# A first batch whose fills are ordered behind its chain: two turned copies, one Square and the routing of three query units

## The chip, the cores and the metric

The kernel runs on one core of a Trainium2 chip. A core has five engines that run their own queues of instructions side by side: TensorE (PE, matmuls; its weight loads are listed apart as PEld), VectorE (DVE), ScalarE (ACT), GpSimd (POOL) and SyncE (SP, which here issues the loads). In the traces of this kernel each queue is worked off in the order in which it was written at build time; an instruction whose inputs are not there yet holds up all that stands behind it on its engine. The metric is the device time of one execution in microseconds, median of the runs.

## The reference, cut to what matters

The shapes are B = 4 batches, N = 11456 tokens of C = 128 numbers, 49 agents, and 8 experts of 128 x 1024 and 1024 x 128 weights.

```python
def sm(a, b):
    s = scale * (a @ b.transpose(0, 2, 1))
    e = np.exp(s - s.max(-1, keepdims=True))
    return e / (e.sum(-1, keepdims=True) + 1e-09)
agent_v = sm(agents, k) @ v                 # 49 rows per batch
x = (sm(q, agents) @ agent_v).reshape(B * N, C)
...
xn, en = x / |x|, expert_emb / |expert_emb|
logits = xn @ en.T / tau
expert_idx, gate_w = argmax(logits), softmax(logits) at it
out = gate_w * (relu(x @ w1[expert_idx]) @ w2[expert_idx])
```

Every x of a batch is a mix of the same 49 rows of agent_v, so nearly all tokens of a batch go to one expert, and the kernel works with `w1.T @ agent_v` (1024 x 49) in place of `w1`. Tokens for which that does not hold are done again at the end.

## The kernel before, in words

Work on keys and queries goes by units of 1024 tokens (8 columns of 128; `NU` = 12 per batch, the last one short). The feed-forward layers go by tiles of 512 tokens (`ffn_mm1`, `ffn_mm2`, `ffn_out`), two to a unit.

`first()` runs the first batch up to the point where its tokens can flow: all key units (`k1_f32`: transposes into PSUM `fTp`, copies to `fT`, scores `sp`, running maximum `m_run`), all value units, the agents' values (`av_chain`), then the **chain** of `pick_expert(0)`. Around the chain stand **fills**, which it does not need: four query units of the first batch (`q_unit(0, 0..3)`, `LEAD` = 4) and six key units of the second batch (`k1_f32(1, 0..5)`).

The chain, with the names that the rows carry: `gp` = w1 times the agents' values on PE; the Square of `w1s` on ACT with its sum (`sel,wsq`), summed over partitions by PE (`total`) and made into a scale on DVE (`hsc`, `sgw`); `gts` = the scaled `gp`, on ACT; from it a key for each of the 1024 hidden columns (`mean`, `pw` over ACT's squares `sel<-gts`, several small steps on `key`, `uid`); `sel<-ident,key` spreads the keys on a diagonal (L729, "the diagonal" below); `row` is PE's product that puts all keys in each partition, copied by ACT; four comparisons on DVE (L747) and four Signs on ACT (L749) count each column's `rank`; eight `sel<-iotaf,rank` (L755) make a selection; `placed` (L763, two times eight matmuls) takes the 256 columns that matter in order, giving `gh` and `gl`. Then `second()` (Square of `w2s` with its sum, a scale, a scaled copy), `linp` and `w2pp`, which give `lin` and `w2p`. With `gh`, `gl` the first layer (`hp`) can start, with `lin`, `w2p` the second (`yp`).

A query unit: transposes and scores as for keys, `qe` (exp), halves in `e_0`/`e_1`, a transpose of them by PE (`tp`, f32 units only, that is the four of `LEAD`), ACT's **turned copy** `tt<-tp`, then **routing**: PE's `rtp` (16 pairs of matmuls), `rtg`, products and sums (`rt`, `qq`) on DVE and POOL, and per group of units (unit 0, units 1 and 2, ...) a row of small steps (`route_group`: `nrm` with a power on POOL, `cc`, `lga`, `ex`, `esa`, `el`, `gs`).

The order of each engine's queue is made at build time by a scheduler that goes by its own timeline and by priorities; `tc.high_priority()` puts a stretch of code ahead, and

```python
    def in_place(last):

        return tc.issue_after(last[-1].ins) if last else nullcontext()
```

keeps what is written inside it behind a given instruction. SP's queue alone is written by hand. Tiles are reused: four PSUM buffers `h` (`fTp`, `tp`, `rtp`, `hp`), two `s` (`sp`), one `rt` buffer for all units.

Of the kernel before, what the change touches and what calls it, by code (L numbers as in the profile page):

```python
# [13 lines left out]
AF = mybir.ActivationFunctionType  # L14
# [4 lines left out]
P = 128  # L19
# [10 lines left out]
def kernel(ctx: ExitStack, tc: tile.TileContext, q, k, v, agents, emb, tau, w1, w2, out):  # L30
    nc = tc.nc
    pe, dve, act, pool, sp = nc.tensor, nc.vector, nc.scalar, nc.gpsimd, nc.sync

    B, N, C = q.shape
    A = agents.shape[1]
    E, D, F = w1.shape
    NF = F // P
# [52 lines left out]
    def psh(name):  # L90
        return ps_h.tile([P, 512], F32, name=name, tag="h")
# [103 lines left out]
    for b in range(B):  # L195
        t_ = pss("aT")
# [91 lines left out]
    gts = cst.tile([P, NF, 2, LO], F32, name="gts")  # L288
    gt16 = cst.tile([P, 2, NF, 2, LO], F16, name="gt16")
    sel = cst.tile([P, NF, FW], F16, name="sel")  # L290
# [79 lines left out]

    DMA_STEPS = 10
    y_log = []
    y_last, h_last, p_last, q_last = [], [], [], []
    h_slots = slots(XS)
    x_slots, s_slots, d_slots, e_slots, t_slots, qe_slots = slots(XB), slots(NU), slots(len(kds)), slots(len(e16)), slots(TB), slots(LEAD)

    def in_place(last):

        return tc.issue_after(last[-1].ins) if last else nullcontext()
# [248 lines left out]
    def pick_expert(b, g):  # L628

        bt = batches[b]  # L630
# [19 lines left out]
        w1s, w2s = load_expert(e0i)  # L650
# [41 lines left out]
        if b > 0:  # L692
            yield 1
            gp = first_layer()
        act.activation(gts[:, :, :, :A], gp[:, : NF * A].rearrange("p (c a) -> p c a", a=A).unsqueeze(2).broadcast_to([P, NF, 2, A]), AF.Copy, scale=sgw)
        yield g

        def second():

            act.activation(w2x[:, :, 0], w2s, AF.Square, accum_out=sq[1])  # L700
            s3, i3 = yield from half_scale(total(sq[1], psx), 6, "w2")
            yield g
            act.activation(w2x[:, :, 0], w2s, AF.Copy, scale=s3)
            if b > 0:
                pool.tensor_tensor(out=w2s, in0=w2s, in1=s3.unsqueeze(2).broadcast_to([P, NF, D]), op=ALU.mult)
                pool.tensor_tensor(out=w2x[:, :, 1], in0=w2s, in1=w2x[:, :, 0], op=ALU.subtract)
            return s3, i3
# [51 lines left out]
        def placed(h, w):  # L759
            t_ = psx("placed")[:, :w]  # L760
            with in_place(y_last):
                for c in range(NF):
                    pe.matmul(out=t_, lhsT=gt16[:, h, c].rearrange("p h a -> p (h a)"), rhs=sel[:, c, :w],  # L763
                              start=(c == 0), stop=(c == NF - 1))
            return t_

        gmx = sm.tile([P, 2], F32, name="gmx", tag="gmx")
# [24 lines left out]
        t_ = psx("linp")  # L792
# [62 lines left out]
    def q_unit(b, u, g):  # L855
        bt = batches[b]
        p, n = ushape(u)
        yield from here(("q", b, u))
        tt_of[b, u] = yield from take(t_slots, len(checks(b, u)) + sum(unit_of(t)[0] == u for t in range(NT)))
        f32 = b == 0 and u < LEAD  # L860
        i = yield from take(x_slots)
        with in_place(p_last) if p_last else behind(asked["q", b, u]):
            xT = pe_T(units["q", b, u], p, n)
        used("q", b, u)
        yield g[0]
        s = pss("sp")
        scores(s, xT, b, p, n)
        give(x_slots, i)
        spv = s[:p, : n * A].rearrange("p (c a) -> p c a", a=A)
        mx = sm.tile([P, UJ], F32, name="qmx", tag="qmx")[:p, :n]  # L870
        dve.tensor_reduce(out=mx, in_=spv, axis=AX.X, op=ALU.max)
        ie = yield from take(qe_slots)
        e = wk.tile([P, UJ, A], F32, name="qe", tag="qe", bufs=LEAD)[:p, :n]
        dve.tensor_tensor(out=e, in0=spv, in1=mx.unsqueeze(2).broadcast_to([p, n, A]), op=ALU.subtract)  # L874
        yield g[1]
        act.activation(e, e, AF.Exp, scale=SCALE)
        yield g[2]
        i = yield from take(e_slots)
        e2 = e16[i % len(e16)]
        hi = e2[:p, :n, :A]  # L880
        i_ = act.copy(hi, e)  # L881
        if not ffn_at[0]:
            q_last[:] = [i_]
        (dve if f32 else pool).tensor_tensor(out=e2[:p, :n, LO : LO + A], in0=e, in1=hi, op=ALU.subtract)  # L884
        tt = wk.tile([P, UJ * P], F16, name="tt", tag="tt", bufs=TB)
        if f32:
            tp = psh("tp").bitcast(F16)
            for c in range(n):
                pe.transpose(out=tp[:, c * p : (c + 1) * p], in_=e2[:p, c, :], identity=ident16[:p, :p])
            act.copy(tt[:, : n * p], tp[:, : n * p])  # L890
        else:
            if ffn_at[0]:
                yield 4
            sp.dma_start_transpose(out=tt[:, : n * p].rearrange("k (c p) -> k c p", p=p),
                                   in_=e2[:p, :n, :].rearrange("p c k -> p (c k)"))
        give(e_slots, i)
        yield g[3]
        tts[b, u] = tt
        while not hasattr(bt, "r_hi"):
            yield 1  # L900
        s = (pss if ffn_at[0] else psh)("rtp")
        with in_place(y_last):
            for c in range(n):
                o = s[:p, c * RW : (c + 1) * RW]
                pe.matmul(out=o, lhsT=tt[:, c * p : (c + 1) * p], rhs=bt.r_hi, start=True, stop=False)
                pe.matmul(out=o, lhsT=tt[:, c * p : (c + 1) * p], rhs=bt.r_lo, start=False, stop=True)
        gi = group_of[u]
        us = groups[gi]
        if (b, gi) not in rtgs:
            rtgs[b, gi] = wk.tile([P, GC, E + 1], F32, name="rtg", tag="rtg", bufs=4)  # L910
        if not hasattr(bt, "qq"):
            bt.qq = sm.tile([P, 2, NCOL], F32, name="qq", tag="qq")
        rtg, qq = rtgs[b, gi], bt.qq
        c0 = ucol(u) - ucol(us[0])
        cs = slice(c0, c0 + n)
        if p < P:
            pmem(rtg[p:, cs], 1.0)
            pmem(qq[p:, :, ucol(u) : ucol(u) + n], 1.0)
        sv = s[:p, : n * RW].rearrange("p (c w) -> p c w", w=RW)
        rt = wk.tile([P, 2, UJ, A], F32, name="rt", tag="rt", bufs=1)[:p, :, :n]  # L920
        act.copy(rtg[:p, cs], sv[:, :, : E + 1])
        pool.tensor_tensor(out=rt[:, 1], in0=e, in1=e, op=ALU.mult)
        dve.tensor_tensor(out=rt[:, 0], in0=sv[:, :, E + 1 :], in1=e, op=ALU.mult)  # L923
        give(qe_slots, ie)
        yield 1
        pool.tensor_tensor(out=rt[:, :, :, : A // 2], in0=rt[:, :, :, : A // 2], in1=rt[:, :, :, A // 2 + 1 :], op=ALU.add)  # L926
        yield g[4]
        dve.tensor_reduce(out=qq[:p, :, ucol(u) : ucol(u) + n], in_=rt[:, :, :, : A // 2 + 1], axis=AX.X, op=ALU.add)
        routed[b, gi] = routed.get((b, gi), 0) + 1
        if routed[b, gi] == len(us):  # L930
            spawn(route_group(b, gi, sum(ushape(x)[1] for x in us)), 1, half=True)
# [520 lines left out]
    def first():  # L1452
# [38 lines left out]
        yield from fetch(two)  # L1491
        for u in range(2):
            spawn(q_unit(0, u, (1, 0, 0, 1, 0)))
        while len(tts) < 2:
            yield 1
        p_last.clear()
        with tc.high_priority():
# [179 lines left out]
```

## Time and profile before

| | us |
|---|---|
| median of 3 runs (lowest, highest) | 740.89 (738.49, 745.61) |
| profiled execution, its own time | 741.78 |
| its span from first to last instruction | 740.0 |
| outside the span | 1.78 |
| PE busy in the span | 688.6 |
| mean granted clock of TensorE, share of full | 0.972 |

The page gives busy times of the engines and the chain that ended last. A view by stretches of time (windows) gives busy time of each engine and the granted clock in each; the timeline lists the instructions of one engine in order, with the idle time ahead of each and what ended it. A matmul in f32 stands as two rows in the trace where the program has one, so 16 `sp` of one unit are x32. Starts are what queues are read by: ends of matmuls are modelled.

### The profile page before, as it was taken

To read this page: it belongs to the slowest core of one execution; us is meant where nothing else is said; L and a number is where in the kernel's file an instruction comes from. 1 tells how busy PE (TensorE), PEld (TensorE's weight loads), DVE (VectorE), ACT (ScalarE), POOL (GpSimd) and SP (SyncE) were. 2 spreads that over 40 slices of the span, in tenths; PEclk is the share of its full clock that TensorE was granted. 3 is DMA by queue.
4 is the path that set the end of the run, shared out by engine and by line. 5 is a ranking of instruction groups with operands and counts; after the bars stand their busy time and mean duration, and the time that the engine had idled before them with its cause. 6 is when DMAs were issued, how large, how long until landed. Compare 5 with 4: busy or idle time off the path is not lost.

```text
span 740.0 us, 23507 instructions
## 1 busy us (share of the span) xinstructions
PE 688.6 (93%) x9416; PEld 574.9 (78%) x9416; DVE 568.1 (77%) x1499; ACT 475.6 (64%) x1161; POOL 338.8 (46%) x576
## 2 busy tenths in 40 slices
PE   8997889989978899999999889989999999999996
PEld 6886678867867788788888778878897776787675
DVE  4676887864457999988558998965658899789886
ACT  3436858667457757877758837865669447766772
POOL 5003401572245557655615836565638356255410
PEclk9998999999969999999999999999999999999998
DMA  8986239846389786598659439945452247223211
GB/s 329 278 306 215 94 73 249 187 137 197 95 205 342 154 199 166 148 279 214 160 158 268 112 67 253 287 124 159 135 172 94 81 87 194 62 60 115 61 45 64
DMA packets 157817, 122.59 MB, mean 166 GB/s; under 512 B 78727, under 2 KB 134105, under 8 KB 157707
## 3 DMA queue, kind: packets, MB, share of 16 engines
q1 hardware_dynamic: 144331, 97.44, 51.1%
q10 hardware_dynamic: 13120, 23.47, 9.1%
q8 instruction: 74, 1.21, 0.7%
q14 instruction: 36, 0.29, 0.1%
q0 software_dynamic: 256, 0.17, 0.1%
HBM read 79.14 MB, written 23.72 MB: 139 GB/s over the span
## 4 chain that ended last, share of the span: by engine, by line
PE 56%; DVE 23%; DMA 6%; ACT 5%; issue 4%; POOL 4%; SPq 0%; ACTq 0%; POOLq 0%; DVEq 0%
PE sp L430 8%; PE fTp L417 6%; PE avp L521 6%; PE hp L1168 4%; PE hp L1169 4%; PE yp L1192 3%; PE yp L1201 3%; DVE hh L1178 3%; PE yp L1204 3%; PE yp L1206 3%; PE yp L1205 3%; PE vp L1017 3%; DMA kt<-in_k_dram 2%; DVE ot L1220 2%; DMA xq<-in_q_dram,ix 1%
## 5 line engine op out<-in xcount | busy, mean ns | idle before, releaser
L1026 ACT ACTIVATE vp<-vp 128x512 f32<-128x512 f32 x191 | 112.3, 588 | 31.7 <-PE vp L1014 16.3
L1178 DVE SCALAR_TENSOR_TENSOR hh<-hp,hh 128x512 f16<-128x512 f32 (+1 forms) x147 | 98.4, 675 | 24.5 <-ACT hh L1177 23.9
L1204 PE MATMUL yp<-w2p,hh 128*128 128x128 f16 (+1 forms) x582 | 109.9, 220 | 0.0
L1205 PE MATMUL yp<-w2p,hh 128*128 128x128 f16 (+1 forms) x582 | 109.8, 220 | 0.0
L1206 PE MATMUL yp<-w2p,hh 128*128 128x128 f16 (+1 forms) x582 | 108.5, 220 | 0.0
L1177 ACT ACTIVATE hh<-hp 128x512 f16<-128x512 f32 (+1 forms) x147 | 85.1, 587 | 34.9 <-PE hp L1169 28.7
L430 PEld LDWEIGHTS sp<-aT_all,fT 128*64 128x64 f32 (+1 forms) x2400 | 83.7, 140 | 23.2 <-issue 11.5
L430 PE MATMUL sp<-aT_all,fT 128*64 128x49 f32 (+1 forms) x2400 | 97.6, 228 | 3.8 <-DVE qe L874 1.4
L1168 PE MATMUL hp<-tt,gh 128*128 128x512 f16 (+1 forms) x207 | 77.5, 377 | 4.3 <-DVE fT L420 2.4
L1169 PE MATMUL hp<-tt,gl 128*128 128x512 f16 (+1 forms) x207 | 77.8, 378 | 0.0
L965 POOL TENSOR_TENSOR nrm<-qq,half 128x16 f32<-128x16 f32 (+2 forms) x28 | 70.4, 2515 | 0.3
L884 POOL TENSOR_TENSOR e<-qe,e 128x392 f16<-128x392 f32 (+1 forms) x44 | 38.1, 866 | 68.0 <-ACT e L881 67.8
L1220 DVE TENSOR_TENSOR ot<-yp,gs 128x512 f32<-128x512 f32 (+1 forms) x92 | 61.1, 670 | 9.3 <-PE yp L1206 3.7
L1201 PE MATMUL yp<-w2f,hh 128*128 128x128 f32 (+1 forms) x456 | 66.7, 284 | 0.0
L1192 PE MATMUL yp<-lin,tt 128*128 128x128 f16 x720 | 63.3, 221 | 2.9 <-DVE w2p L810 1.4
L1204 PEld LDWEIGHTS <-hh 128*128 128x128 f16 (+1 forms) x582 | 57.6, 99 | 10.3 <-issue 0.5
L422 ACT COPY fT<-fTp 128x512 f32<-128x512 f32 (+1 forms) x87 | 48.6, 563 | 24.7 <-PE fTp L417 17.9
L1206 PEld LDWEIGHTS <-hh 128*128 128x128 f16 (+1 forms) x582 | 57.5, 99 | 8.1 <-issue 1.5
L1205 PEld LDWEIGHTS <-hh 128*128 128x128 f16 (+1 forms) x582 | 57.4, 99 | 5.8 <-issue 0.3
L1201 PEld LDWEIGHTS yp<-w2f,hh 128*128 128x128 f32 (+1 forms) x456 | 58.9, 194 | 2.9 <-issue 1.1
L926 POOL TENSOR_TENSOR rt<-rt 128x384 f32<-128x384 f32 (+1 forms) x48 | 40.5, 843 | 45.1 <-DVE rt L923 42.0
L417 PE MATMUL fTp<-ident,qt 128*128 128x128 f32 x360 | 57.0, 288 | 3.3 <-ACT fT L422 1.1
(373 smaller groups left out, 1786.3 us busy)
## 6 DMA issues: line engine op xcount, KB each, us to landing
kt<-in_k_dram SPq DMA_DIRECT2D x44, 512.0 KB, 6.6
vt<-in_v_dram SPq DMA_DIRECT2D x44, 512.0 KB, 6.2
qt<-in_q_dram SPq DMA_DIRECT2D x44, 512.0 KB, 5.5
out_dram<-ot ACTq DMA_DIRECT2D x88, 256.0 KB, 3.4
w1s<-in_moe_w_dram SPq DMA_DIRECT2D x8, 512.0 KB, 4.6
w2s<-in_moe_w_dram SPq DMA_DIRECT2D x8, 512.0 KB, 5.6
tt<-e SPq DMA_TRANSPOSE x44, 4.1
kt<-in_k_dram SPq DMA_DIRECT2D x4, 96.0 KB, 5.8
```

What stands on the lines that cost most here:

```text
L417: pe.transpose(out=tp[:, c * p : (c + 1) * p], in_=src[:p, c0 + c, :], identity=ident[:p, :p])
L430: pe.matmul(out=s[h : h + w, c * A : (c + 1) * A], lhsT=xT[:, c * p + h : c * p + h + w], rhs=aT_all[:, b, :], start=True, stop=True, skip ...
L1026: act.activation(z[:p], z[:p], AF.Relu, scale=-1.0, accum_out=bt.vsum[:p, at : at + 1])
L1168: pe.matmul(out=hp[:, :m], lhsT=bt.gh[:, fs], rhs=tt, start=True, stop=False)
L1169: pe.matmul(out=hp[:, :m], lhsT=bt.gl[:, fs], rhs=tt, start=False, stop=True)
L1177: h_last[:] = [act.activation(hh[:, :m], hp[:, :m], AF.Relu)]
L1178: dve.scalar_tensor_tensor(out=hl[:, :m], in0=hp[:, :m], scalar=0.0, in1=hh[:, :m], op0=ALU.max, op1=ALU.subtract)
L1192: pe.matmul(out=yp[:p, c, :], lhsT=tc_, rhs=bt.lin[:, h], start=(c == 0 and h == 0), stop=False, skip_group_check=True)
L1201: y_last[:] = [pe.matmul(out=y, lhsT=hh[:, cs], rhs=bt.w2f[:, f], start=False, stop=last, skip_group_check=True)]
L1204: pe.matmul(out=y, lhsT=hh[:, cs], rhs=wh, start=False, stop=False, skip_group_check=True)
L1205: pe.matmul(out=y, lhsT=hh[:, cs], rhs=wl, start=False, stop=False, skip_group_check=True)
L1206: y_last[:] = [pe.matmul(out=y, lhsT=hl[:, cs], rhs=wh, start=False, stop=last, skip_group_check=True)]
```

## The change

It makes three edits, all of which concern the first batch alone.

1. The instruction that makes `gts` is kept in `bt.marks`. The turned copies of the four f32 query units, and in batch 0 the Square of `w2s`, are written behind it on ACT.
2. The last `placed` matmul is kept in `bt.placed`. The `rtp` matmuls of query units 1 to 3 are written behind it on PE (unit 0 stays free).
3. Since the turned copies now wait for the chain, `first()` goes on to the chain when the first two units have their casts (`cast`), no longer when they have their turned copies (`tts`).

```diff
-        act.activation(gts[:, :, :, :A], gp[:, : NF * A].rearrange("p (c a) -> p c a", a=A).unsqueeze(2).broadcast_to([P, NF, 2, A]), AF.Copy, scale=sgw)
+        i_ = act.activation(gts[:, :, :, :A], gp[:, : NF * A].rearrange("p (c a) -> p c a", a=A).unsqueeze(2).broadcast_to([P, NF, 2, A]), AF.Copy, scale=sgw)
+        bt.marks = [i_]
...
-            act.activation(w2x[:, :, 0], w2s, AF.Square, accum_out=sq[1])
+            with in_place(bt.marks if b == 0 else []):
+                act.activation(w2x[:, :, 0], w2s, AF.Square, accum_out=sq[1])
...
-                    pe.matmul(out=t_, lhsT=gt16[:, h, c].rearrange("p h a -> p (h a)"), rhs=sel[:, c, :w],
-                              start=(c == 0), stop=(c == NF - 1))
+                    i_ = pe.matmul(out=t_, lhsT=gt16[:, h, c].rearrange("p h a -> p (h a)"), rhs=sel[:, c, :w],
+                                   start=(c == 0), stop=(c == NF - 1))
+            bt.placed = [i_]
...
+            cast.append(u)
...
         if f32:
+            while not hasattr(bt, "marks"):
+                yield 1
...
-            act.copy(tt[:, : n * p], tp[:, : n * p])
+            with in_place(bt.marks):
+                act.copy(tt[:, : n * p], tp[:, : n * p])
...
+        while f32 and u > 0 and not hasattr(bt, "placed"):
+            yield 1
         s = (pss if ffn_at[0] else psh)("rtp")
-        with in_place(y_last):
+        with in_place(bt.placed if f32 and u > 0 else y_last):
...
-        while len(tts) < 2:
+        while len(cast) < 2:
             yield 1
```

What stands in the queues changes only in the first third of the program: SP's queue is the same row for row, and PE, DVE, ACT and POOL come back to the order of before after 23 to 30 in 100 of their rows; from the product `placed` for the matrix `vm` on the differences are shifts by a few rows.

ACT around `gts` before, from the cast of the second query unit on (`sel,wsq<-w1s` is the Square of w1, `w1s,wsq<-w2s` that of w2, `tt<-tp` a turned copy):

```order
L881 CAST e_1_150<-qe 128x8x49
L688 ACTIVATE sel,wsq_1030<-w1s 128x1024
L700 ACTIVATE w1s,wsq_1031<-w2s 128x8x128
L890 COPY tt<-tp 128x1024
L921 COPY rtg<-rtp 128x72
L695 ACTIVATE gts<-gp,sgw 128x16x49
L921 COPY rtg<-rtp 128x72
L711 ACTIVATE sel<-gts 128x392
L733 CAST gt_152<-gts 128x16x49
```

and now, in the same place (the first turned copy stood two rows further up before):

```order
L884 CAST e_1_150<-qe 128x8x49
L688 ACTIVATE sel,wsq_965<-w1s 128x1024
L422 COPY fT<-fTp 128x512 x2
L695 ACTIVATE gts<-gp,sgw 128x16x49
L897 COPY tt<-tp 128x1024 x2
L702 ACTIVATE w1s,wsq_966<-w2s 128x8x128
L713 ACTIVATE sel<-gts 128x392
L735 CAST gt_152<-gts 128x16x49
```

Two turned copies and the Square of w2 moved from ahead of `gts` to the place between `gts` and its squares, and two copies of query transposes moved ahead of it.

PE before, ahead of and between the first `placed` matmuls (`kt` are keys of the second batch):

```order
L417 MATMUL fTp<-ident,kt 128x128 x4
L430 MATMUL sp<-aT_all,fT 64x49 x8
L417 MATMUL fTp<-ident,kt 128x128 x4
L430 MATMUL sp<-aT_all,fT 64x49 x8
L417 MATMUL fTp<-ident,kt 128x128 x4
L763 LDWEIGHTS gt_152
L763 MATMUL placed<-sel,gt_152 128x256
```

and now, from the last fill ahead of `row` to the first of the sixteen `placed`, which follow each other:

```order
L915 LDWEIGHTS tt
L915 MATMUL rtp<-r_lo,tt 128x58
L430 MATMUL sp<-aT_all,fT 64x49 x25
L742 MATMUL row<-sel,ones 128x512 x2
L765 LDWEIGHTS gt_152
L765 MATMUL placed<-sel,gt_152 128x256
```

Between `row` and the first `placed` stood before eight `tp`, 32 `rtp` matmuls, the transposes of three key units and the scores of one and a half, and between the sixteen `placed` further ones. Now nothing stands there, and all of it comes behind the sixteenth `placed`, ahead of the first `yp`. From the second `tp` group of the stretch to the first `yp` PE has the same set of matmuls in both orders, but for one small `mT`.

DVE now, from the diagonal to the rank (`cc` takes POOL's `nrm`, `esa` ACT's `ex`, `gs` POOL's `el`):

```order
L731 TENSOR_TENSOR sel<-ident,key 128x1024
L733 TENSOR_SCALAR nkey<-key 128x8
L877 TENSOR_TENSOR qe<-sp,qmx 128x392
L937 TENSOR_REDUCE qq<-rt 128x2x8
L406 COPY m_run<-sp 128x392
L888 TENSOR_TENSOR e_1_150<-qe,e_1_150 128x8x49
L983 RECIPROCAL cc<-nrm 128x8
L749 TENSOR_SCALAR sel,rank<-sel,key 128x1024 x2
L991 TENSOR_REDUCE esa<-ex 128x8
L749 TENSOR_SCALAR sel,rank<-sel,key 128x1024
L998 RECIPROCAL gs<-el 128x8
L749 TENSOR_SCALAR sel,rank<-sel,key 128x1024
```

The sum `qq` of unit 0 and the steps `cc`, `esa`, `gs` of group 0 stood ahead of the comparisons before, `qq` and `cc` even ahead of the diagonal; now `cc` stands right ahead of the four comparisons and `esa` and `gs` between them.


## Rows read from the trace of the kernel before

**Rows 1.** The chain that ended last, two pieces: start us, us, what

```profile
64.70 0.94 ACT gts L695
...
90.52 0.98 PE placed L763 x8
```

**Rows 2.** Windows: stretch, length, busy us (instructions) of PE, PEld, DVE, ACT, POOL; clock, DMA

```profile
61.90:102.30 40.40, 34.45 (x472) 27.60 (x472) 34.49 (x95) 31.45 (x63) 15.78 (x27) 0.94 0.25 84
109.00:300.00 191.00, 178.17 (x2528) 150.31 (x2528) 139.73 (x321) 127.61 (x307) 89.67 (x150) 0.96 0.75 195
300.00:740.00 440.00, 416.96 (x5577) 346.63 (x5574) 350.87 (x948) 290.47 (x739) 220.44 (x347) 0.99 0.54 141
```

**Rows 3.** Windows again, short ones, for the granted clock (third figure from the end)

```profile
50.00:53.00 3.00, 3.00 (x16) 3.00 (x17) 1.28 (x6) 0.58 (x1) 0.00 (x0) 0.50 0.52 209
53.00:54.00 1.00, 1.00 (x10) 0.98 (x10) 0.38 (x2) 0.56 (x1) 0.00 (x0) 0.84 0.85 180
60.00:61.00 1.00, 0.00 (x0) 0.00 (x0) 0.00 (x0) 0.91 (x3) 0.00 (x0) 0.57 0.99 401
62.00:67.00 5.00, 4.70 (x51) 4.55 (x50) 2.64 (x10) 4.71 (x11) 1.69 (x5) 0.50 0.02 9
67.00:68.00 1.00, 1.00 (x9) 0.71 (x7) 1.00 (x3) 0.85 (x2) 0.69 (x1) 1.00 0.00 0
```

**Rows 4.** Timeline of PE: start us, us, line, out<-in, count, idle before it and releaser

```profile
61.87 1.03 PE L889 MATMUL tp<-ident,e 128*128 128x128 f16 x8 [2.76 <-DVE e L884]
...
63.35 0.56 PE L252 MATMUL total<-wsq,ones 128*128 128x1 f32 x2
...
65.15 2.98 PE L417 MATMUL fTp<-ident,qt 128*128 128x128 f32 x16
...
72.96 1.14 PE L430 MATMUL sp<-aT_all,fT 128*64 128x49 f32 x32 [1.35 <-DVE qe L874]
...
76.14 1.98 PE L740 MATMUL row<-sel,ones 128*128 128x512 f32 x4 [0.51 <-DVE sel L729]
...
90.45 1.05 PE L763 MATMUL placed<-sel,gt 128*128 128x256 f16 x8
...
102.29 0.23 PE L1192 MATMUL yp<-lin,tt 128*128 128x128 f16 x1 [1.43 <-DVE w2p L810]
```

**Rows 5.** Timeline of ACT, the same columns

```profile
62.28 1.06 ACT L700 ACTIVATE w1s<-w2s 128x1024 f16<-128x1024 f32 x1
...
63.33 0.99 ACT L890 COPY tt<-tp 128x1024 f16<-128x1024 f16 x1
...
64.70 0.93 ACT L695 ACTIVATE gts<-gp,sgw 128x784 f32<-128x784 f32 x1 [0.25 <-DVE sgw L691]
```

**Rows 6.** Timeline of DVE, the same columns

```profile
65.66 0.56 DVE L712 TENSOR_REDUCE mean<-gts 128x8 f32<-128x392 f32 x1 [0.34 <-ACT gts L695]
...
74.87 1.21 DVE L729 TENSOR_TENSOR sel<-ident,key 128x1024 f32<-128x1024 f32 x1
...
78.78 1.28 DVE L747 TENSOR_SCALAR_CACHE_REDUCE sel<-sel,key 128x1024 f16<-128x1024 f32 x1 [1.60 <-ACT sel L741]
...
87.48 1.94 DVE L755 TENSOR_SCALAR sel<-iotaf,rank 128x256 f16<-128x256 f16 x6
...
91.70 0.42 DVE L771 CAST gl<-placed 128x256 f16<-128x256 f32 x1
```

**Rows 7.** Source line L755 within 80:95: duration ns min/median/max, first and last start

```profile
L755 DVE TENSOR_SCALAR sel<-iotaf,rank x8: 273/274/958, 84.6 to 89.1; 128x256 f16<-128x256 f16 x8
```

**Rows 8.** Timeline of POOL, the same columns

```profile
67.31 0.84 POOL L922 TENSOR_TENSOR rt<-qe 128x392 f32<-128x392 f32 x1 [0.87 <-DVE qq L928]
...
71.12 0.20 POOL L969 TENSOR_TENSOR nrm<-ls,nrm 128x8 f32<-128x8 f32 x1
...
84.59 0.87 POOL L926 TENSOR_TENSOR rt<-rt 128x384 f32<-128x384 f32 x1 [0.80 <-DVE rt L923]
...
88.31 2.94 POOL L965 TENSOR_TENSOR nrm<-qq,half 128x16 f32<-128x16 f32 x1
```

More of the change, by code (lines that the diff above doesn't have):

```diff
@@ L372 @@
     y_log = []
-    y_last, h_last, p_last, q_last = [], [], [], []
+    y_last, h_last, p_last, q_last, cast = [], [], [], [], []
     h_slots = slots(XS)
```

## The prediction, made before the result was known

> **What bounds the kernel now.** I read the stretches first, then the chain, then the four timelines of the first batch. PE is busy 688.6 of 740 us, so the question is where it stands still. Behind 109 us it idles 12.8 us of 191 and 23.0 of 440 [rows 2]. In the stretch that the change reorders, from PE's second group of turned transposes (61.87) to its first `yp` (102.29) [rows 4], it is busy 34.45 of 40.40 us [rows 2]: 5.95 us idle. The chain that ended last runs through this stretch by way of `gts` and `placed` [rows 1]. Two readings are possible. The chain of the first batch sets when tokens flow; and the fills put around it keep PE at work while DVE and ACT do the chain. The change shortens the first and moves the second, so the sum has to count both. I take as measure the start of the first `yp`, since the set of matmuls ahead of it is the same in both orders.
>
> **Up to `gts`: about 1.0 us later.** ACT loses a turned copy between the two casts, so the second cast, the half that waits for it and the second `tp` group come about 0.45 earlier: 61.4. But PE now puts eight query transposes where seven routing columns stood, ahead of `total`. Sixteen take 2.98 us [rows 4] over a rise of the clock; at the lower level, with the three key and query halves of 50 to 53 us [rows 3] as a check, eight are 1.6 us. `total` starts near 63.9 (63.35 before [rows 4]), and the second query copy, which ACT has ahead of `gts`, waits for four more transposes, to 65.25, and takes 0.6. `gts` starts near 65.75, against 64.70 [rows 5].
>
> **From `gts` to the diagonal: 9.2 us against 10.2.** DVE is full from `mean` to the diagonal, 65.66 to 74.87 [rows 6]. Seven pieces of routing and copying leave this run (two `qq`, one `rt`, one query copy, one `qe`, `cc`, `esa`) and `rmx` joins: five of them are of the size of `mean` (0.56 us [rows 6]), two are small; some 2.6 us less. ACT takes part of that back: two turned copies (0.99 each) and the Square of w2 (62.28 to 63.33, 1.05) [rows 5] now stand between `gts` and its squares, some 2.9 us, and `pw` waits 0.6 us for them; the half of unit 2, which DVE has ahead of the last key step, waits 1 us for a cast that is as late. So the diagonal starts near 74.9, as before (74.87). Bounds: 74.2, if `gts` loses only 0.3; 75.6.
>
> **From the diagonal to `placed`: little gained, and PE stands still.** `row` follows the diagonal by 1.27 us (76.14 to 74.87) [rows 4, 6]: 76.2. Ahead of it PE has 24 transposes, `tp`, `total`, the scores of three units and one unit's routing. With 3 us for 16, 1.14 for one unit's scores [rows 4] and 2 for the rest that is 9.9 us from 61.4, so of 14.8 us it idles **4.9** (0.5 and 1.35 of such waits stood there before). Then nothing stands between `row` and `placed`, and `placed` needs the selection, the selection the rank, the rank four comparisons and four Signs.
>
> The comparisons started at 78.78 [rows 6]. Now `cc` stands ahead of them on DVE and wants POOL's power of unit 0's sum. Before, POOL's first step after that sum started at 67.31 and the last step ahead of `cc` at 71.12 with one foreign 0.9 us piece between [rows 8]; so `cc` comes some 3.3 us after the sum, which ends near 77.2: 80.5. Four comparisons of 1.28 us [rows 6] follow, each with a short read of its sum, with `esa` and `gs` between: the rank is ready near 86.3, the eight selections (1.94 us for six [rows 6]) take until 88.9, and `placed` ends near 90.3, where the last group started at 90.45 and its copy `gl` at 91.70 [rows 4, 6]. The chain gains about 1 us there, at best 3.5 (no wait for `cc`, PE at full clock).
>
> One selection took 958 ns, the others 274 [rows 7]; it started with a POOL addition that ran from 84.59 for 0.87 us [rows 8]. I take 8 x 0.32 = 2.6 us, since POOL has nothing to do there now. The Trainium skill ("SBUF — State Buffer", section "SBUF: two separate sides") says that VectorE in some modes and GpSimd lock one port pair in turn and that the loser "fully blocks". The first selection agrees with that; by that rule alone the later six, beside a POOL instruction of 2.94 us [rows 8], would have stood still too, and with one more such block the rank's end would come 0.7 later.
>
> PE meanwhile idles from the end of `row` (78.0) to the first selection (86.8): **8.8 us**, where fills stood before. If the clock falls in the idle time ahead of `row`, `row` itself takes up to twice its 1.98 us [rows 4], the comparisons start near 81.1, and the idle time is 6.9 of work at the lower level and waiting alike; the end is the same within 0.5. The level fell to 0.50 about a microsecond into the 2.76 us wait of 59 to 61.9 and was back at 67 [rows 3, 4]: after the new wait I count 1.2 us for the second spell, bounds 0 and 2.5.
>
> The Trainium skill ("TensorE: Matmul & The Clock Gate", section "Part 4: PE-mode transpose") says that PE transposes do not bring the full clock. Here the level rose between 53 and 54 us when PE had done sixteen transposes in a row and one small product since 50.6 [rows 3], so the trace speaks against it. By the rule `gts` would come 0.4 us later still, and the first `yp` as much.
>
> **The first `yp`.** 61.4 (start) + 34.45 (the same work) + 4.9 + 8.8 (idle) + 1.2 (second spell of low clock) + 1.4 (the wait for `w2p`, 1.43 before [rows 4]: DVE still has seven selections for `vm` ahead of it) − 0.3 (`mT`, now later) − 0.5 (the spell of low clock and the waits of `placed` for its selections overlap) = 111.4. I take **111.2, 8.9 us later than 102.29** [rows 4]. Everything that was taken out from between `row` and `placed` (routing, transposes and scores of five units) now stands ahead of the first layers, so a `placed` that is 1 us earlier buys nothing. Bounds: +4.4 (`placed` at 88.0 and no low clock) and +11.5.
>
> **Behind it.** From the product for `vm` on the queues are as before, so the delay is carried on; loads move with it (SP's order is unchanged, and the DMA engines have room: busy for 0.25 of their time in the stretch [rows 2]). PE's 35.9 us of idle time behind 109 [rows 2] can swallow some where the wait is for a transfer or for POOL work that was not pushed back; the waits that I can name hang on queues that are pushed back as a whole. I take a tenth off: **+8.0**, bounds of the share half and none. The profiled execution took 741.78, 0.9 over the median 740.89 of the runs; the sum is a difference, and set on the median it gives **749.0**.
>
> **Rivals.**
> (a) *The debt is swallowed in part.* PE's idle time of 109 to 300 us, 12.8 us [rows 2], belongs for the most part to the second batch's chain on DVE, ACT and POOL; if that chain is not pushed back with PE, half of the delay is lost there: +2.5 to +6, about 745. For it: the second batch's chain, like the first's, is a row of small steps on DVE and ACT. Against: the chain begins with a product of all value units, which PE does in order.
> (b) *The chain wins* (the other side). If what decides is when `gh`, `gl` are there, the seven pieces less on DVE bring `placed` from 91.5 to 88.0, and key fills behind it find room later: −3.5, about 737.4. It needs `cc` to be ready when the row copies are (79 us) and over 8 us of debt to be swallowed; the order shows the fills ahead of the first layers, which speaks against it.
> (c) *Worse still:* `cc`, `gs` and the second group's power (2.94 us [rows 8]) hold DVE again between `placed` and `w2p`, the first `yp` comes at 114 or later: +12, 753.
>
> **How the numbers follow.** A measurement of this kernel can tell about 1 per cent, 7.4 us, from no change: the three runs lie within 7.1 us. My forecast (+6 to +11.5, 747 to 752.4) gets 0.62, (a) 0.24, (b) 0.06, (c) 0.08. The forecast lies on both sides of 748.3; some two thirds of it and (c) are slower by over 1 per cent, 0.52; faster by over 1 per cent would need over twice what (b) gives, 0.03; the rest is 0.45. The range leaves out (b) and the top of (c): 743.5 to 752.8.
>
> **What would show it.** Right: `gts` later than 64.7; PE idle for 7 us or more between `row` and `placed`, with the granted clock at 0.50 in 82 to 87; `cc` on DVE waiting for POOL ahead of the first comparison; `gl` between 88.5 and 92; the first `yp` near 111, and the same distance between the two traces at 200, 300 and 700 us. Wrong: a first `yp` before 106, or a distance that shrinks by more than 3 us between 110 and 300.

## The result, and the profile after

| | before | with the change |
|---|---|---|
| median of 20 runs (lowest, highest), us | 741.43 (737.73, 745.61) | 745.53 (742.61, 749.34) |
| ratio, 95% interval | | 1.006 (1.0042 to 1.0079) |
| profiled execution, its span | 741.78, 740.0 | 745.83, 744.1 |
| mean granted clock | 0.972 | 0.965 |

Slower by 4.1 us, between 3.1 and 5.9. One run of e3, 752.79 us, over 1.5 per cent above the fastest of its kernel, counts as slow and is left out of its numbers. The kernel before was timed again beside each group of runs (medians 740.53 to 741.63), and a ratio is to the runs beside it. The page of the changed kernel: busy time by engine, and the granted clock in 40 slices.

```profile
PE 689.4 (93%) x9416; PEld 574.6 (77%) x9416; DVE 567.7 (76%) x1499; ACT 475.6 (64%) x1161; POOL 340.2 (46%) x576
...
PEclk9996799999978999999999999999999999999999
```

PE has the same work. The fourth and fifth slices (56 to 93 us) hold two spells of low clock, about 58 to 71 and 78 to 88 us; the kernel before has one there, 60 to 67 [rows 3]. Windows of the changed kernel between the second `tp` group, `row`, the end of `placed` and the first `yp`:

```profile
58.64:73.33 14.69, 13.67 (x146) 11.78 (x146) 9.21 (x27) 8.55 (x16) 2.72 (x4) 0.57 0.36 119
73.33:87.27 13.94, 5.58 (x24) 3.29 (x25) 11.06 (x34) 7.59 (x15) 4.02 (x9) 0.68 0.00 1
87.27:105.90 18.63, 18.63 (x304) 16.14 (x302) 11.35 (x29) 15.29 (x30) 9.51 (x15) 0.97 0.29 92
```

The same three stretches of the kernel before, which together are the stretch of [rows 2]:

```profile
61.87:76.14 14.27, 11.20 (x170) 9.86 (x171) 11.75 (x34) 10.00 (x21) 8.09 (x14) 0.82 0.34 116
76.14:91.50 15.36, 13.91 (x188) 10.66 (x190) 13.48 (x36) 12.80 (x26) 6.51 (x9) 1.00 0.35 111
91.50:102.29 10.79, 9.37 (x115) 7.10 (x116) 9.25 (x28) 8.68 (x18) 1.17 (x5) 1.00 0.01 2
```

The case is in these rows. From `row` to the end of `placed` PE's instructions fell from 188 to 24, and the stretch became only 1.4 us shorter (15.36 to 13.94). Behind `placed` they rose from 115 to 304, and that stretch became 7.8 us longer, with PE busy in all of it. PE's timeline of the changed kernel has the idle time (rows that answer to [rows 4]):

```profile
55.67 0.62 PE L895 MATMUL tp<-ident,e 128*128 128x128 f16 x8
58.64 1.03 PE L895 MATMUL tp<-ident,e 128*128 128x128 f16 x8 [2.35 <-DVE e L888]
...
61.17 0.42 PE L252 MATMUL total<-wsq,ones 128*128 128x1 f32 x2
...
73.33 1.98 PE L742 MATMUL row<-sel,ones 128*128 128x512 f32 x4 [1.02 <-DVE sel L731]
83.67 3.60 PE L765 MATMUL placed<-sel,gt 128*128 128x256 f16 x16 [8.35 <-DVE sel L757]
...
105.90 0.62 PE L1201 MATMUL yp<-lin,tt 128*128 128x128 f16 x8
...
107.00 0.22 PE L1213 MATMUL yp<-w2p,hh 128*128 128x128 f16 x1 [0.48 <-DVE w2p L813]
...
114.02 0.39 PE L1029 MATMUL vp<-vm,tt 128*128 128x64 f16 x8 [0.64 <-DVE vm L835]
```

DVE and ACT of the changed kernel (answering to [rows 5, 6]):

```profile
71.83 1.44 DVE L731 TENSOR_TENSOR sel<-ident,key 128x1024 f32<-128x1024 f32 x1
...
77.81 0.20 DVE L983 RECIPROCAL cc<-nrm 128x8 f32<-128x8 f32 x1 [1.84 <-POOL nrm L978]
77.93 1.23 DVE L749 TENSOR_SCALAR_CACHE_REDUCE sel<-sel,key 128x1024 f16<-128x1024 f32 x1
...
83.14 1.65 DVE L757 TENSOR_SCALAR sel<-iotaf,rank 128x256 f16<-128x256 f16 x8
...
87.30 0.42 DVE L774 CAST gl<-placed 128x256 f16<-128x256 f32 x1 [0.37 <-PE placed L765]
```

```profile
63.07 0.94 ACT L695 ACTIVATE gts<-gp,sgw 128x784 f32<-128x784 f32 x1
```

PE's queue is the same in both programs up to the first `tp`, and yet that starts 2.8 us earlier with the change. So all distances are taken from it. In the trace of before it stands at 58.49, and a wait for a load, with slower products behind it, says why:

```profile
8.45 1.54 PE L417 MATMUL fTp<-ident,kt 128*128 128x128 f32 x8 [1.75 <-DMA kt<-in_k_dram]
...
58.49 0.62 PE L889 MATMUL tp<-ident,e 128*128 128x128 f16 x8 [0.28 <-DVE e L884]
```

Starts minus the start of the first `tp`, us, with a second trace of each kernel (e7 and e8, below); `foldp` is the first product of the agents' values of batches 2 to 4, "last" the last row of PE's timeline:

| | gts | row | placed | first yp | first vp | foldp 2 | foldp 3 | foldp 4 | last |
|---|---|---|---|---|---|---|---|---|---|
| before | 6.2 | 17.7 | 27.5 | 43.8 | 50.5 | 143.9 | 319.4 | 474.7 | 673.9 |
| before, e7 | 6.2 | 18.3 | 29.1 | 45.4 | 52.1 | 145.5 | 321.0 | 474.5 | 675.9 |
| change | 7.4 | 17.7 | 28.0 | 50.2 | 58.4 | 150.2 | 327.9 | 481.3 | 680.3 |
| change, e8 | 7.3 | 17.4 | 27.7 | 49.9 | 58.0 | 149.8 | 326.1 | 481.7 | 680.7 |

The first pair of traces is 6.4 us apart at the first `yp` and at the end, the second 4.4 and 4.8. The delay is made between `row` and the first `yp` and is carried through the whole program, though it swings by up to 3 us from mark to mark (7.9 and 5.9 at the first `vp`).

### The profile page after: what moved, and what is told of

It is laid out like the page before. It is cut to its first block, busy times and chain, and to the rows that moved or that the text cites. A ratio compares the mean times of both kernels' runs of the same rounds, so it can differ in the third digit from the quotient of the medians.

```text
span 744.1 us, 23511 instructions
## 1 busy us (share of the span) xinstructions
PE 689.4 (93%) x9416; PEld 574.6 (77%) x9416; DVE 567.7 (76%) x1499; ACT 475.6 (64%) x1161; POOL 340.2 (46%) x576
## 4 chain that ended last, share of the span: by engine, by line
PE 52%; DVE 27%; DMA 6%; issue 5%; POOL 5%; ACT 4%; SPq 0%; ACTq 0%; POOLq 0%; DVEq 0%
PE sp L430 7%; PE fTp L417 7%; PE avp L521 6%; DVE hh L1187 3%; PE hp L1177 3%; PE hp L1178 3%; PE yp L1201 3%; DVE sel L749 3%; PE yp L1215 2%; PE yp L1213 2%; PE yp L1214 2%; DVE ot L1229 2%; PE yp L1210 2%; PE vp L1026 2%; PE placed L765 2%
## 5 line engine op out<-in xcount | busy, mean ns | idle before, releaser
L1213 PE MATMUL yp<-w2p,hh 128*128 128x128 f16 (+1 forms) x582 | 108.9, 219 | 0.5 <-DVE w2p L813 0.5
L1214 PE MATMUL yp<-w2p,hh 128*128 128x128 f16 (+1 forms) x582 | 108.8, 219 | 0.0
L1215 PE MATMUL yp<-w2p,hh 128*128 128x128 f16 (+1 forms) x582 | 107.2, 219 | 0.1
L1229 DVE TENSOR_TENSOR ot<-yp,gs 128x512 f32<-128x512 f32 (+1 forms) x92 | 61.1, 669 | 10.3 <-PE yp L1210 3.6
L888 POOL TENSOR_TENSOR e<-qe,e 128x392 f16<-128x392 f32 (+1 forms) x44 | 38.1, 866 | 67.4 <-ACT e L884 67.2
L935 POOL TENSOR_TENSOR rt<-rt 128x384 f32<-128x384 f32 (+1 forms) x48 | 40.5, 844 | 50.5 <-DVE rt L932 47.7
```

The source lines that it names most:

```text
L1213: pe.matmul(out=y, lhsT=hh[:, cs], rhs=wh, start=False, stop=False, skip_group_check=True)
L1214: pe.matmul(out=y, lhsT=hh[:, cs], rhs=wl, start=False, stop=False, skip_group_check=True)
L1215: y_last[:] = [pe.matmul(out=y, lhsT=hl[:, cs], rhs=wh, start=False, stop=last, skip_group_check=True)]
```

## The experiments

The theory (A): edit 2 takes PE's fills out of the time that DVE and ACT need between `row` and `placed`; PE stands still there and does them later. The main rival (B): the turned copies and the Square of w2, which now stand between `gts` and its squares on ACT, are the price. A third (C): the low clock that follows the idle time.

**e1: edit 2 undone.**

```diff
-        while f32 and u > 0 and not hasattr(bt, "placed"):
-            yield 1
         s = (pss if ffn_at[0] else psh)("rtp")
-        with in_place(bt.placed if f32 and u > 0 else y_last):
+        with in_place(y_last):
```

> The change without its second edit: turned copies and the Square of w2 stay behind gts, but the routing of units 1 to 3 is free again, and the queue has 16 rtp, 16 tp, 12 groups of key transposes and most of their scores between row and placed. Theory A (the price is PE standing still between row and placed, because edit 2 took the fills out): idle time of PE between row and the first placed under 2 us in place of 8.35, first yp 44 to 46 us behind the first tp (43.8 before, 50.2 with the change), time 739 to 743 us. Theory B (the price is the two turned copies and the Square on ACT between gts and its squares, or a gts that comes later): nothing is won back, 744 to 747 us, diagonal and row as late as with the change.

Measured 739.15 us, ratio to before 0.9978 (0.9957 to 1.0000). Its window from `row` to the end of `placed`, and its first `yp`:

```profile
73.18:88.55 15.37, 12.58 (x168) 10.06 (x164) 14.78 (x37) 13.94 (x30) 11.87 (x19) 1.00 0.31 86
```

```profile
98.89 0.61 PE L1198 MATMUL yp<-lin,tt 128*128 128x128 f16 x8 [0.87 <-DVE lin L800]
```

168 instructions stand in the gap again, the clock is full, and the first `yp` comes 43.3 behind the first `tp` (55.58). PE's idle time there is 2.8 us, not under 2 as expected, and the first `yp` a little earlier than the 44 to 46 expected. B is out: ACT has the turned copies and the Square where the change has them, `gts` starts at 7.3 as with the change, and the loss is gone. Edit 2 costs 745.53 − 739.15 = 6.4 us (4.9 by e12); by the ratios, which take each kernel against its own neighbours, 6.1 and 5.2.

**e2: edit 2 alone** (the lines of e1 the other way, on the kernel before).

> Edit 2 alone: turned copies and the Square as before, the routing of units 1 to 3 behind the last placed. The queue then has nothing between unit 0's routing and row, and nothing between row and placed: the transposes of two query units, key work and scores of three units all stand behind. Theory A: PE idles some 8 us ahead of row and some 8 us ahead of placed, the first yp comes 54 to 60 us behind the first tp, time 748 to 756 us. Theory B: gts and diagonal come as before or earlier, placed 2 to 4 us earlier, and the time is 738 to 742 us. A third possibility, the delay being swallowed behind the first yp: idle times as in A and a time of 743 to 747.

Measured 751.53 us, 1.0144 (1.0103 to 1.0185). Its PE:

```profile
68.87 3.67 PE L740 MATMUL row<-sel,ones 128*128 128x512 f32 x4 [7.60 <-DVE nkey L731]
79.06 3.57 PE L763 MATMUL placed<-sel,gt 128*128 128x256 f16 x16 [6.52 <-DVE sel L755]
...
116.62 0.58 PE L1023 MATMUL vp<-vm,tt 128*128 128x64 f16 x8 [0.64 <-DVE vm L833]
```

The chain is much shorter: `row` 13.2 behind the first `tp` (55.67) and `placed` 23.4, 4.1 earlier than before. The first `vp` is at 61.0, 10.5 later, and the kernel 11 us slower (751.53 − 740.53, the median of before beside it). (Its first `yp` came at 38.1, not at the 54 to 60 expected: it is one early group, and most of the work that stood ahead of it before comes behind it, so `vp` is the mark here.)

**e3: the turned copies alone** (edits 1 and 3 without the Square and without edit 2).

> Edit 1 for the turned copies with edit 3, without the Square and without the routing; the Square of w2 stands ahead of the query copies again. Theory A: fills stand between row and placed as before; time 739 to 743 us, and the same as the change without edit 2 within 1.5. Theory B: two thirds of the price of ACT's three instructions is left, 743 to 746 us.

Measured 744.61 us (median of eleven runs), 1.0051 (1.0024 to 1.0078): a miss for A, and by its number B's. But its first `vp` comes at 105.84, 50.0 behind the first `tp`, as in e1 (50.3), and `foldp` 2 at 143.6 in both. The loss comes later: 1.7 us over e1 at `foldp` 3, 3.4 at `foldp` 4, 3.6 at the end. Unlike e1, whose PE queue is that of before again after 16 in 100 of its rows, this one differs up to half of the program, and there PE has a wait that the other traces lack:

```profile
333.94 0.59 PE L1173 MATMUL hp<-tt,gh 128*128 128x512 f16 x1 [2.69 <-DVE hh L1183]
```

Between 240 and 340 us behind the first `tp` PE idles 4.5 us in all, in e1 1.45. So this run says little about ACT in the first batch; what it shows is a small edit there that goes with another order up to half of the program, and with a loss of some 3 us over 200 us further on. That the order makes the loss is a reading of these waits; no run tests it.

**e4: the clock held up.** On the changed kernel, behind the second `row` product:

```diff
+            if b == 0 and h == 1:
+                t_ = psx("warm")
+                with in_place([i_]):
+                    for _ in range(26):
+                        pe.matmul(out=t_, lhsT=ident16, rhs=ident16.unsqueeze(1).broadcast_to([P, 4, P]), start=True, stop=True)
```

> The change, with 26 matmuls of 512 f16 columns on a constant between row and the first placed on PE, whose result nobody reads. They take 5.5 us at the full clock and hold nothing up unless the clock is low already. Theory A: the wait itself is the price and the low clock behind it (78.6 to 88.5 with the change) only a small part: the granted clock stays at 1.00 until placed, placed (3.60 us with the change) takes about 2.0, and the time is 743.5 to 745, one to two under the change. Theory C (the low clock that follows the idle time is the price): 740 to 742.5 us. If they only delay placed: 746 to 749.

Measured 744.90 us, 0.6 under the change and inside A's range; C falls. The products did their work:

```profile
77.17 5.78 PE L748 MATMUL warm<-ident 128*128 128x512 f16 x26
84.02 1.92 PE L770 MATMUL placed<-sel,gt 128*128 128x256 f16 x16 [1.08 <-DVE sel L762]
...
104.08 0.62 PE L1206 MATMUL yp<-lin,tt 128*128 128x128 f16 x8
```

`placed` takes 1.92 us in place of 3.60 and the clock is full behind it. But the products fill the wait with nothing of use. In the trace the first `yp` comes 2.8 us earlier than with the change (47.4 behind the first `tp` at 56.66, against 50.2), and still 3.6 and 2.0 later than in the two traces before; at the end 0.7 of that is left (679.5 against 680.3). In the medians it is 0.6, which the intervals of the two ratios don't tell from nothing (1.0026 to 1.0073 and 1.0042 to 1.0079). So the low clock has a share in the delay at the first `yp`, but giving the clock back gives back little of the time.

**e5: the `rtp` tiles of units 1 to 3 from another PSUM pool.** Which part of what edit 2 moved is the price? It names the routing; but with it the key transposes left the gap too. They take tiles from the same four `h` buffers in turn, and a tile that waits for `placed` blocks those behind it.

```diff
-        s = (pss if ffn_at[0] else psh)("rtp")
+        s = (psy if f32 and u > 0 else pss if ffn_at[0] else psh)("rtp")
```

> The change, with one word altered: the rtp tiles of units 1 to 3 are taken from the two y buffers of PSUM in place of the four h buffers, in which the key transposes rotate too. Routing of units 1 to 3 stays behind the last placed. In the queue 8 tp, 40 key transposes and their scores now stand between row and the first placed; only the 48 rtp pairs stand behind it. Theory A1 (the price is not the routing that edit 2 names, but the key work that it held back, because a tile of h that waits for placed blocks the rotation): PE idles under 3.5 us between row and placed in place of 8.35, and the time is 738 to 742 us, as without edit 2. Theory A2 (routing behind placed is the price, since it delays the first layers or DVE's work on vm): 743.5 to 747 us.

Measured 748.35 us, 1.0091 (1.0056 to 1.0126), outside both ranges. The keys did come back into the gap, but now the routing held the two `y` buffers, from which the chain's own later products come:

```profile
8.17 1.97 PE L417 MATMUL fTp<-ident,kt 128*128 128x128 f32 x8 [1.83 <-DMA kt<-in_k_dram]
...
59.35 0.62 PE L895 MATMUL tp<-ident,e 128*128 128x128 f16 x8
...
102.59 2.94 PE L797 MATMUL linp<-w2s,gts 128*128 128x128 f32 x16 [3.21 <-DVE rt L932]
```

A new wait took the place of the old one, so it tells A1 and A2 not apart. The number is no evidence against A1 either: in this trace the first `tp` stands 3.7 us later than in that of the change (59.35 against 55.67), where both queues are still the same, and counted from it e5 ends 1.1 us earlier than the change (679.2 against 680.3; first `vp` 54.2 against 58.4). Why its six runs lie 3 us over the change is not settled. e9 asks the same question without changing pools.

**e6: the small steps of group 0 behind `gl`.**

```diff
+        while b == 0 and gi == 0 and not hasattr(bt, "glc"):
+            yield 1
+        with in_place(bt.glc if b == 0 and gi == 0 else []):
-        dve.reciprocal(cc, nrm)
+            dve.reciprocal(cc, nrm)
```

> The change, with the three small steps of group 0 (cc, esa, gs on DVE, and with them ex on ACT) behind gl in place of ahead of and between the comparisons. PE's queue is the same instruction for instruction. Theory A with the wait for POOL as a part of it: the first comparison starts some 1.8 us earlier behind row (2.7 us in place of 4.6), the selections and placed 2 us earlier, PE's idle time between row and placed falls from 8.35 to 6 to 6.8, and all of that arrives at the end, since PE has nothing else to do there: 743 to 744.3 us. Rival (b) of the prediction in its own terms (a chain that comes earlier is what decides): the same start, and more than it, 741 to 743. If the small steps only move their wait to the time between placed and w2p: 745 to 747.

Measured 745.23 us, 1.0044 (1.0018 to 1.0069): no gain that can be told, and the number of the third outcome, though not by its mechanism. In its trace the clock fell ahead of `row`, which took 3.78 us, and the first comparison waited for `row`'s copies where it had waited for POOL:

```profile
73.10 3.78 PE L742 MATMUL row<-sel,ones 128*128 128x512 f32 x4 [3.42 <-DVE sel L731]
83.32 3.59 PE L765 MATMUL placed<-sel,gt 128*128 128x256 f16 x16 [6.43 <-DVE sel L757]
```

```profile
77.54 1.28 DVE L749 TENSOR_SCALAR_CACHE_REDUCE sel<-sel,key 128x1024 f16<-128x1024 f32 x1 [1.80 <-ACT sel L743]
```

`row` to `placed` takes 10.2 us here, 10.3 with the change and 10.3 in e8. With `row` as slow as here, the first comparison starts 4.4 us behind `row`'s start without the wait for POOL and 4.6 with it (e8). What the wait is worth behind a quick `row` and an idle PE this trace does not show.

**e7 and e8: the two kernels once more**, one trace each.

> The kernel before once more, for how far two traces of the same program differ. If the 2.8 us by which its first tp came later than in the other five traces (58.49 against 55.6 to 56.7) is chance, it comes between 55.5 and 57 here and the span is 736 to 740; if it belongs to the program, at 58 to 59. The low clock behind the first tp: 4 to 13 us long in the other traces, so anything in that is expected.

> The changed kernel once more. PE's idle time between row and placed 8 to 8.8 us again. If the low clock behind the second tp is 13 us long again, row has some 1 us of idle time ahead of it; if it ends within 6 us, some 4 to 5 us, as the prediction had it, with row at the same place within 0.7. First yp 49 to 51 us behind the first tp either way.

e7: span 743.6; the first `tp` is late again (59.33), behind a wait of 1.76 us for the second `kt` load. By the expectation that would belong to the program; but e5, whose queue on PE is that of the change up to there, has the same wait. e8: span 746.1, first `tp` at 56.74, and

```profile
74.10 3.78 PE L742 MATMUL row<-sel,ones 128*128 128x512 f32 x4 [3.42 <-DVE sel L731]
84.44 3.60 PE L765 MATMUL placed<-sel,gt 128*128 128x256 f16 x16 [6.55 <-DVE sel L757]
```

The idle time between `row` and `placed` is 6.55, not 8 to 8.8 as expected: `row` took at the low clock what PE idled in the first trace, and both together are 10.3 in either.

**e9 and e10: the keys asked for first.** Edits and pools as in the change; the routing of a unit asks for its tile only when some key units of batch 2 are in the program (two for units 1 and 2, three for unit 3; in e10 three for unit 2 as well).

```diff
-        while f32 and u > 0 and not hasattr(bt, "placed"):
+        while f32 and u > 0 and not (hasattr(bt, "placed") and batches[1].__dict__.get("blks") and batches[1].blks[0].k1 >= (2,2,2,3)[u]):
```

> The change, with the routing of units 1 and 2 not asked for a tile of h until two key units of the second batch have been put into the program, and that of unit 3 not until three have. All edits stay, all tiles stay in the buffers of the change; routing of units 1 to 3 stands behind placed as with the change, and from the product for vm on PE's queue is that of the change. But 8 tp, 24 key transposes and 40 to 56 scores stand between row and placed, and linp is asked for behind two units' routing at most. Theory A1 (the price is the key work that edit 2 held back through the rotation of h): PE idles under 4 us between row and placed in place of 8.35, the first yp comes 43.5 to 47 us behind the first tp (50.2 with the change, 43.8 before), time 738 to 742 us. Theory A2 (routing behind placed is itself the price, by what it does to DVE and to vm): the gap is filled, first yp at 48 or later, 744 to 748 us.

> The same with unit 2 put behind three key units as well: two of the three routings then come later than linp has been asked for. Theory A1: as e9 within 1.5 us, 738 to 742. Theory A2: 744 to 749, and over e9, since more of the routing is late.

Measured 742.96 us, 1.0022 (0.9998 to 1.0047), and 744.28, 1.0031 (1.0008 to 1.0053): e9 lies between the two ranges, e10 at the lower end of A2's. e9's stretch from `row` to the end of `placed`, and the wait that is left:

```profile
73.15:91.50 18.35, 13.74 (x184) 10.73 (x185) 12.21 (x36) 13.74 (x27) 3.83 (x9) 0.91 0.21 65
```

```profile
102.04 0.61 PE L1201 MATMUL yp<-lin,tt 128*128 128x128 f16 x8
...
104.05 0.22 PE L1213 MATMUL yp<-w2p,hh 128*128 128x128 f16 x1 [1.41 <-DVE w2p L813]
```

A1's marks in the trace are met: 184 instructions stand there again, the waits ahead of the first `placed` sum to 3.6 us, and the first `yp` comes 46.5 behind the first `tp` (55.59), with all 48 `rtp` matmuls of units 1 to 3 (16 a unit) still behind `placed`. In time 2.6 us of the change's 4.1 are back, but the intervals of the two ratios overlap. In the traces 4.5 are back at the end (last at 675.7 behind the first `tp`, 680.3 with the change, 673.9 and 675.9 before); at the first `vp` less, 55.0 against 58.4 with the change and 50.5 and 52.1 before. So key work that edit 2 never names is part of the price, by the medians and by the ends of the traces the larger part; its share is not settled. What remains, 1.3 us and 2.7 in e10, may be the late routing (A2); that is not shown. The first `yp` products wait for `w2p` or `lin`, 1.41 here and 2.21 in e10, but such a wait stood there in the kernel before too (1.43 [rows 4]). The interval of e9 doesn't exclude that nothing remains.

**e11: e1 with e6's edit; e12: e1 again.**

> The change without its second edit, and with the three small steps of group 0 behind gl as in e6: does what bought nothing with an idle PE buy anything when fills cover the chain? If PE is the bound there, as theory A says, an earlier placed changes nothing: 738 to 741 us, the same as e1 within 1.5. If the chain decides once the fills are back: 736 to 738.

> The kernel of e1 again, whose interval against the kernel before ended at 1.0000. If edits 1 and 3 alone are worth something (a shorter chain, 0.5 to 2 us), the ratio is 0.996 to 0.999 again; if e1 was luck in when the first loads land, 0.999 to 1.002.

Measured 741.29 us, 1.0002 (0.9971 to 1.0033), and 740.66, 0.9990 (0.9958 to 1.0021). With fills in the gap the small steps are worth nothing that can be told (e11 and e12 are 0.6 us apart), and edits 1 and 3 alone are level with the kernel before: 0.9990 stands on the border of the two outcomes, and e1's gain was not seen again. Of these versions none beats it by more than can be measured.

## Why the prediction was right in sign and cause, and too high

The cause stood: PE idle between `row` and `placed`, its work pushed behind, carried to the end. The size did not: 749.0 against 745.53, +8.0 against +4.1. The measured time lies below the forecast's own 747 to 752.4; that it lies inside the whole range, 743.5 to 752.8, is owed to the room left for rival (a), whose mechanism was not seen, and so to luck. Of the three outcomes the likeliest, slower by over 1 per cent, did not come; the ratio is within it.

Of its signs, PE's idle time (8.35 us), the clock of 0.50 in 82 to 87 and the wait of `cc` for POOL are there. Three are times of the trace, and miss: `gts` at 63.07 (later than 64.7 was named), `gl` at 87.30 (88.5 to 92) and the first `yp` at 105.90, just ahead of the 106 below which the prediction called itself wrong. The trace stands 2.8 us earlier from the first `tp` on; set to the first `tp` of before, the three are 65.9, 90.1 and 108.7.

- *`gts` 1.0 later:* 1.2 and 1.1 in the two traces. *The diagonal as before:* 0.2 earlier (16.2 behind the first `tp`, 16.4 before), with 8.8 us from `gts` where 9.2 were worked out. e1 shows that none of this reaches the end.
- *`cc` ahead of the comparisons, 1 us gained by the chain:* `cc` waited 1.84 us for POOL, and `placed` ended 1.4 earlier in its distance from the first `tp` (31.6, 33.0 before), forecast 31.8. The price of the wait was right. Whether it costs anything on its own is open: e6 is no faster without it, but there a slow `row` held the comparisons in its place.
- *The selections:* 2.6 us forecast, 1.65 measured, none of the eight slow as in [rows 7]. POOL is all but idle then. The Trainium skill ("SBUF — State Buffer", section "SBUF: two separate sides") says that VectorE in some modes and GpSimd hold one port pair in turn; this trace doesn't speak against it, with no POOL instruction between 81.3 and 89.0, but can't test it for the same reason.
- *4.9 us of idle time from the second `tp` group to `row`:* 1.02 in the first trace, 4.5 in e6 and 3.6 in e8 (3.42 of it right ahead of `row` in both). In the first the clock stayed at 0.50 for some 13 us and the fills took 13.67 us, in e6 9.65 (forecast 9.9), so that PE worked where it would have waited. `row` is at 17.3 to 17.7 in all three.
- *8.8 us ahead of `placed`:* 8.35, or 6.5 with a slow `row`, as the prediction's own sentence on a slow `row` had it.
- **The step that was mis-sized is the sum for the first `yp`.** From the second `tp` group to it 49.8 us were forecast (61.4 to 111.2) and 47.26 measured: 2.5 less (47.0 in e8). The wait for `w2p` (1.4) was not there ahead of it; 0.48 of it comes one group later, and the reading is that PE's longer work behind `placed` covers DVE. Idle time and low clock were put at 4.9 + 8.8 + 1.2 − 0.5 = 14.4 us; measured are 9.37 of idle time and 3.44 more of busy time than 34.45 (37.89), 12.8. The work at low clock and the waiting cover each other more than the 0.5 that was taken off.

```profile
58.64:105.90 47.26, 37.89 (x470) 31.21 (x471) 31.61 (x89) 31.43 (x60) 16.25 (x27) 0.76 0.23 74
```

- *A tenth swallowed:* none. The distance between the traces is 6.4 at the first `yp`, 6.3, 8.5 and 6.6 at the three `foldp`, 6.4 at the end; in the second pair 4.4, then 4.3, 5.1, 7.2, 4.8. The time is that of rival (a), but its mechanism was not seen.
- The rest, from 6.4 or 4.8 in the traces to 4.1 in the medians, is not settled. Both traces of the kernel before had a late first load; if it is late oftener in that program, it adds to the time before and hides part of the loss, though nothing in the queues says why it should be, and e5, a version of the change, had it too.

## What to carry to other kernels

Work that fills an engine's wait must be counted where it goes, not only where it leaves: e2 has a chain 4.1 us shorter and is 11 us slower, since the work that no longer fills PE's waits comes behind them, where PE has next to no idle time to give (1.9 of the 34 us from the end of `placed` to the first `vp`). When an instruction is ordered behind a late one, look which buffer it asks for: what takes the next buffers of the same pool in turn is ordered with it, and moves though no line of the edit names it; in e5 and e9, where the late routing no longer held `h` ahead of the keys, they went back into the gap. A small edit can also change the order far from it (e3), so compare distances at several marks before putting a difference down to the place of the edit.

## What the runs showed of the hardware

The same instructions got the full clock back at very different times. Windows of the change: PE busy throughout, and the second spell, which is the idle time ahead of `placed`.

```profile
59.00:70.00 11.00, 11.00 (x97) 9.23 (x94) 5.91 (x19) 7.91 (x14) 0.00 (x0) 0.50 0.36 109
...
71.00:72.00 1.00, 1.00 (x34) 1.00 (x31) 1.00 (x5) 0.00 (x0) 0.84 (x2) 0.80 0.25 98
...
79.00:88.00 9.00, 4.33 (x34) 3.34 (x35) 8.15 (x29) 3.67 (x7) 0.45 (x2) 0.50 0.00 1
```

And of e6, whose PE queue is the same row for row:

```profile
59.00:61.00 2.00, 2.00 (x14) 2.00 (x15) 0.00 (x0) 0.45 (x3) 0.00 (x0) 0.50 0.17 68
61.00:62.00 1.00, 1.00 (x9) 1.00 (x8) 0.31 (x1) 0.42 (x1) 0.00 (x0) 0.64 0.00 0
62.00:63.00 1.00, 1.00 (x21) 0.78 (x20) 0.93 (x6) 0.59 (x1) 0.00 (x0) 1.00 0.52 74
```

The full clock is back after some 3 us there and after some 13 in the trace of the change; in e3 it did not fall at all in this stretch, though PE waited 2.49 us for the same tile. From the second `tp` group (58.91) on PE does that group, twelve query transposes and, after eight of them, one `total` (61.45), so e6 has the clock rise between 61 and 62 with little but transposes behind it. The Trainium skill ("TensorE: Matmul & The Clock Gate", section "Part 4: PE-mode transpose") says that they do not bring the full clock; e6 speaks against it (0.50 until 61, 1.00 from 62), and the difference between two traces with the same instructions is one that the rule does not tell.

The landing of one early load moves all that follows: the first `tp` starts between 55.58 and 59.35 us in the fourteen traces, latest in the three where the second `kt` load held PE for 1.75 to 1.83 us (both of the kernel before, and e5).
